# Attention and two feed-forward layers on one core: output groups six blocks behind, next pair's weights in sequence, its input parts behind product 7

## The chip, the cores and the metric

The kernel runs on one core of one Trainium2 chip. The metric is device time in microseconds (us), the median over several executions. Five engines each work through a queue of their own in order: TensorE (PE, matmuls), VectorE (DVE), ScalarE (ACT), GpSimd (POOL) and SyncE (SP, which here issues every DMA transfer).

## The reference

```python
def reference(**kwargs):
    attn_out = _attn_ref(**attn_kwargs)        # causal, window 128, 4 x 8 heads x 576 x 64
    x = np.ascontiguousarray(attn_out.transpose(0, 2, 1, 3)).reshape(B * S, H * D)   # 2304 x 512
    x = _moe_ref(x=x, **moe_kwargs)            # (silu(x @ w_gate) * (x @ w_val)) @ w_out, 1536 wide
    return _moe2_ref(x=x, **moe2_kwargs)       # h = x @ w_in; (h * tanh(softplus(h))) @ w_out, 2048 wide
```

All of it is fp32. The first feed-forward layer is called layer 1 below, the second layer 2.

## The kernel before

Every fp32 operand of a large matmul is kept as two halves, a high one that ACT writes (a copy to the type fp32r, `hi_act`) and a low one that DVE writes (the difference, `lo_dve`). One logical matmul is three on PE: high x high, high x low, low x high.

**Layer 1** runs over five chunks of tokens (`A_CHUNKS`, the last has 384). For each of 12 blocks of the hidden width, `gv_groups` makes 24 matmuls into two of four rotating PSUM banks (gate and value; ACT and DVE read them and write the halves `hh`, `hl`), and `out_group` makes 12 matmuls that add the block to the four output banks `acc0` to `acc3`. Output groups run some blocks behind: the last chunk's by `CFG["lastlag"]`. Those that are left when the last block is done (the list `carry`) run on PE just before layer 2. Their weights come in six `ring` tiles of two blocks each, read back from DRAM (`cw<-w1od`) and split by ACT and DVE; two of them fit at a time. After the last output group the four banks are copied out (`ev`).

While the last chunk runs, `combos` prepares layer 2's output weights for eight column blocks: it loads one (`cw<-w2d`), takes four differences on POOL, splits seven parts into halves (`chl`, ACT and DVE) and stores them to DRAM (`w2o<-chl`).

**Layer 2** takes 2x2 blocks by seven products in place of eight (a scheme of the Strassen kind), in three pairs of 384-token tiles. Per pair, `hidden` is called for j = 0 to 7, each with seven products of six matmuls on the input's seven parts `xs1` to `xs7` and the weight tile `win` of j. `make_win` makes `win`: four differences on POOL in the one tile `t4`, then high and low halves by ACT and DVE, in two pieces of 768 and 1024 columns, from the raw weights that `load_raw` fetches (`w<-w2d`, two buffers). Then come the output products in the order `ORDER2` = 4, 1, 6, 7, 2, 5, 3. Each consists of four operands `op` (halves of the hidden values `G`; five buffers) and 12 matmuls per operand, with weights `wout` loaded 1 MB at a time into three buffers. `x_parts` makes the next pair's `xs` from `xr`, its input as loaded from `x2d`: seven high halves on ACT, seven low halves on DVE and four sums on DVE. `win` and `xr` take turns in three buffers of one tag.

PE's order is the program's own. The queues of the other engines are filled by a scheduler that takes what its own clock says is ready first; the kernel gives it priorities and, with `tc.issue_after`, single orders. In the loop over pairs `x_parts` and `make_win` of the next pair stand among the output products:

```python
if p + 1 < NPB:
    if i == 7:
        xs = x_tiles(br, range(1, 8))
        x_parts(xs, xr)
    if i in (2, 5):
        j = (2, 5).index(i)
        make_win(p + 1, j)
        load_raw(p + 1, j + 2)
```

Of the kernel before, what the change touches and what calls it, by code (L numbers as in the profile page):

```python
# [9 lines left out]
F32 = mybir.dt.float32  # L10
F32R = mybir.dt.float32r
# [3 lines left out]
AF = mybir.ActivationFunctionType  # L15
ALU = mybir.AluOpType
# [8 lines left out]
A_CHUNKS = [512, 384, 512, 512, 384]  # L25
S_FULL = [4, 4, 0, 0, 0]
TB = 384
NPB = NT // (2 * TB)
NJ = NF2 // 2

SLOT = {1: 0, 2: 1, 3: 2, 5: 3, 6: 4, 7: 5, 4: 6}
CFG = dict(
    order="SSOTT", delay0=2, early=[4], pbufs=10, pump_g=2, pump_p=2, lag=4, lastlag=3, evprio=500,
    conv_a=0.1, conv_b=0.9,
)

# [60 lines left out]
def body(ctx: ExitStack, tc: tile.TileContext, qT, kT, vP, w1, w1o, w2, cst, yT):  # L97
    nc = tc.nc
# [10 lines left out]
    w2d = dr.tile([NF2, 128, 1024], F32, name="w2d")  # L109
# [11 lines left out]


    def hi_act(out, in_):
        nc.scalar.activation(out=out, in_=in_, func=AF.Copy)  # L124

    def lo_dve(out, in_, hi):
        nc.vector.tensor_tensor(out=out, in0=in_, in1=hi.bitcast(F32), op=ALU.subtract)  # L127

    plansA = []
    t = 0  # L130
# [165 lines left out]
    early = {}  # L296
# [219 lines left out]
    def conv_w2(i):  # L516
# [10 lines left out]

        steps(("w2d", i), [f0] + [lambda k=k: raw["f"][k]() for k in range(5)] + [f6])

    def combos(b):  # L530

        st = {}

        def f0():
            st["w"] = bpool["p"].tile([128, 8, 256], F32, tag="cw8", name="cw8")
            nc.sync.dma_start(out=st["w"][:, 0:4], in_=w2d[b].rearrange("p (k n) -> p k n", k=4))

        def f1():
            w = st["w"]
            for o, x, y in ((4, 0, 1), (5, 3, 4), (6, 3, 0), (7, 5, 2)):  # L540
                nc.gpsimd.tensor_tensor(out=w[:, o], in0=w[:, x], in1=w[:, y], op=ALU.subtract)  # L541

        def half(e):
            st[e] = bpool["p"].tile([128, 7, 256], F32R, tag="chl", name="chl", bufs=3)
            return st[e]

        def f2():
            hi_act(half(0), st["w"][:, 1:8])

        def f3():  # L550
            lo_dve(half(1), st["w"][:, 1:8], st[0])

        def f4():
            for e in range(2):
                h = st[e].bitcast(F32)
                nc.sync.dma_start(out=w2o[:, :, b - NJ, e].rearrange("s p n -> p s n"), in_=h)

        steps(("c", b), [f0, f1, f2, f3, f4])
# [34 lines left out]
    def gv_groups(ci, i):  # L593
        p = plansA[ci]
        n = p.n
        st = {}

        def g():
            need(("w", i))
            st["g"] = hid(x_t[ci], n, wt[i], 0)  # L600
            t = hp_.tile([128, 512], F32, tag="t", name="t")
            tanhs.append(nc.scalar.activation(out=t[:, :n], in_=st["g"][:, :n], func=AF.Tanh, scale=0.5))  # L602
            nc.vector.scalar_tensor_tensor(  # L603
                out=t[:, :n], in0=t[:, :n], scalar=1.0, in1=st["g"][:, :n], op0=ALU.add, op1=ALU.mult
            )
            st["t"] = t

        def v():
            vps = hid(x_t[ci], n, wt[i], 512)
            t = st["t"]  # L610
            nc.vector.scalar_tensor_tensor(  # L611
                out=t[:, :n], in0=t[:, :n], scalar=0.5, in1=vps[:, :n], op0=ALU.mult, op1=ALU.mult
            )
            if ci == len(plansA) - 1:
                hh = bpool["p"].tile([128, 512], F32R, tag="hhb", name="hh", bufs=CFG["lastlag"] + 2)
                hl = bpool["p"].tile([128, 512], F32R, tag="hlb", name="hl", bufs=CFG["lastlag"] + 2)
            else:
                hh = hp_.tile([128, 512], F32R, tag="hh", name="hh", bufs=2)
                hl = hp_.tile([128, 512], F32R, tag="hl", name="hl", bufs=2)
            hi_act(hh[:, :n], t[:, :n])  # L620
            lo_dve(hl[:, :n], t[:, :n], hh[:, :n])
            hs["A", ci, i] = (hh, hl)

        return [g, v]
# [29 lines left out]
    def bank():  # L654
# [3 lines left out]
            return rot("bk")  # L658
        return ps.tile([128, 512], F32, tag=f"acc{c % CT}", name="bk", bufs=1)

    def part(x, src):
        hi_act(x[:, 0], src)
        lo_dve(x[:, 1], src, x[:, 0])

    def add(out, a, b, op=ALU.add):
        nc.vector.tensor_tensor(out=out, in0=a, in1=b, op=op)  # L666
# [20 lines left out]
    def x_tiles(bp, which):  # L687
        return {i: bp.tile([128, 2, 2, TB], F32R, tag=f"xs{i}", name=f"xs{i}", bufs=1) for i in which}
# [50 lines left out]
    def layer2(br):  # L739
# [9 lines left out]
        def load_raw(p, j):  # L749
            raws[p, j] = br.tile([128, 4, 256], F32, tag="w4", name="w4", bufs=2)  # L750
            nc.sync.dma_start(out=raws[p, j], in_=w2d[j].rearrange("p (k n) -> p k n", k=4))

        def make_win(p, j):

            w = raws.pop((p, j))
            x = t4
            for o, a, b in ((0, w[:, 0], w[:, 1]), (1, w[:, 3], x[:, 0]), (2, w[:, 3], w[:, 0]), (3, x[:, 1], w[:, 2])):
                nc.gpsimd.tensor_tensor(out=x[:, o], in0=a, in1=b, op=ALU.subtract)  # L758
            t = win[p, j] = br.tile([128, 2, 7, 256], F32R, tag="win", name="win")
            for d, src in ((slice(0, 3), w[:, 1:4]), (slice(3, 7), x)):  # L760
                hi_act(t[:, 0, d], src)
                lo_dve(t[:, 1, d], src, t[:, 0, d])
# [62 lines left out]
        for p in range(NPB):  # L825
            loads = [(i, k) for i in ORDER2 for k in range(2)]
            for j in range(NJ):
                if j + 2 < NJ:
                    make_win(p, j + 2)
                if j + 4 < NJ:  # L830
                    load_raw(p, j + 4)
                if j >= NJ - 3:
                    load_wout(p, *loads.pop(0))
                hidden(p, j, xs)
            if p + 1 < NPB:
                xr = load_x(br, p + 1)
                for j in range(2):
                    load_raw(p + 1, j)
            us = [{}, {}]
            ys = [[bp.tile([128, 2, TB], F32, tag="y", name="y", bufs=4) for _ in range(2)] for _ in range(2)]  # L840
            held = {}
            left = [[2, 2], [2, 2]]
            t0 = 2 * p * TB
            for i in ORDER2:
                bks = held[i] = held[onto2[i]] if i in onto2 else [bank(), bank()]
                for q, o in enumerate(operands(p, i)):
                    k, jq = divmod(2 * q, NJ // 2)
                    if (p, i, k) not in wout:
                        load_wout(p, i, k)
                        loads.remove((i, k))  # L850
                    w = wout[p, i, k]
                    if jq == 0 and loads:
                        load_wout(p, *loads.pop(0))
                    for m in range(2):
                        products(
                            bks[m],
                            [(w[:, jq + e, 0, 128 * m:128 * m + 128], w[:, jq + e, 1, 128 * m:128 * m + 128]) for e in range(2)],
                            [(o[:, 0, e], o[:, 1, e]) for e in range(2)],
                            i not in onto2 and q == 0, i not in onto2.values() and q == NJ // 2 - 1,
                        )  # L860
                for m in range(2):

                    def done(k, a, b, m=m):
                        t, f = divmod(k, 2)
                        y = ys[f][m]
                        if b is None:
                            nc.scalar.activation(out=y[:, t], in_=a, func=AF.Copy)
                        else:
                            add(y[:, t], a, b, ALU.subtract if k == 2 else ALU.add)
                        left[f][m] -= 1  # L870
                        if not left[f][m]:
                            nc.sync.dma_start(out=yr[:, 2 * f + m, t0:t0 + 2 * TB], in_=y.rearrange("p a t -> p (a t)"))

                    def new():
                        return bp.tile([128, TB], F32, tag="u", name="v", bufs=6)

                    if i == 4:
                        us[m]["p4"] = bks[m][:, :TB]
                        continue
                    outputs(i, bks[m], us[m], new, done, False)  # L880
                    if i == 7:
                        done(2, us[m]["b"], us[m]["p4"])
                if p + 1 < NPB:
                    if i == 7:
                        xs = x_tiles(br, range(1, 8))
                        x_parts(xs, xr)
                    if i in (2, 5):
                        j = (2, 5).index(i)
                        make_win(p + 1, j)
                        load_raw(p + 1, j + 2)  # L890

    with tc.manual_schedule(engines={mybir.EngineType.PE}):
        nc.sync.dma_start(out=cst_sb, in_=cst)
# [162 lines left out]
```

## Time and profile before

| what | value |
| --- | --- |
| median of 3 runs | 1024.19 us (1022.73 to 1025.08) |
| the profiled execution | 1022.81 us, of which the span of the trace is 1021.0 us |
| TensorE busy | 982.3 us, 96% of the span |
| VectorE busy | 704.1 us, 69% |
| ScalarE busy | 550.5 us, 54% |
| GpSimd busy | 183.2 us, 18% |
| mean granted TensorE clock | 0.986 of full |

A group of the trace's rows gives start, duration, engine, line and the tiles written and read; in square brackets stands the idle time of the engine before it and what ended that. The granted clock is a share of TensorE's full speed.

### The profile page before, as it was taken

How to read it: one execution, taken by the hardware profiler on the slowest of the kernel's cores; microseconds unless marked ns; L12 is line 12 of the kernel's file. 1: busy time of each engine (PE TensorE's matmuls, PEld its weight loads, DVE VectorE, ACT ScalarE, POOL GpSimd, SP SyncE). 2: the span in 40 equal slices, each digit the busy share in tenths (PEclk: the TensorE clock that was granted, in tenths of full speed). 3: DMA queues.
4: the chain of work that ended last, by engine and by line, in shares of the span. 5: the costliest groups of instructions: out<-in, count | busy, mean ns of one | idle time of the engine just before them, and what ended most of it. 6: DMA issues, size and time to landing. Idle time of an engine off the chain costs nothing.

```text
span 1021.0 us, 14513 instructions
## 1 busy us (share of the span) xinstructions
PE 982.3 (96%) x5168; PEld 861.5 (84%) x5168; DVE 704.1 (69%) x1247; ACT 550.5 (54%) x1121; POOL 183.2 (18%) x204
## 2 busy tenths in 40 slices
PE   7899999999999999999999999599999999999998
PEld 5566777899987777787888999599899998999998
DVE  5988887777667644558643666877974888757773
ACT  6867565767666654545543345456453564335442
POOL 3700000000000000000002342542821429113000
PEclk9989999999999999999999999799999999999999
DMA  8844423476354622336401997513685236850275
GB/s 314 287 193 134 158 80 115 146 245 204 84 186 142 225 84 61 110 111 235 159 22 63 329 367 257 210 63 104 226 288 187 83 121 231 292 160 21 69 258 189
DMA packets 74936, 173.90 MB, mean 170 GB/s; under 512 B 8432, under 2 KB 50032, under 8 KB 65136
## 3 DMA queue, kind: packets, MB, share of 16 engines
q1 hardware_dynamic: 74864, 172.98, 51.0%
q8 instruction: 40, 0.66, 0.2%
q14 instruction: 32, 0.26, 0.1%
HBM read 137.30 MB, written 35.65 MB: 169 GB/s over the span
## 4 chain that ended last, share of the span: by engine, by line
PE 77%; DVE 8%; DMA 5%; POOL 5%; ACT 2%; issue 2%; SPq 1%; DVEq 0%; ACTq 0%; POOLq 0%
PE g_ps L117 28%; PE bk L117 24%; PE acc L117 14%; PE o_ps L117 5%; POOL t L758 4%; PE s_ps L117 4%; PE t_ps L259 3%; DMA wout<-w2o 2%; DVE G L666 1%; DVE win L127 1%; DMA wraw<-w 1%; DVE op L127 1%; POOL Pt L249 1%; DVE xs L127 1%; DVE xr L666 1%
## 5 line engine op out<-in xcount | busy, mean ns | idle before, releaser
L117 PE MATMUL g_ps<-xt,w 128*128 128x512 f32 (+1 forms) x1440 | 322.2, 375 | 0.3 <-ACT PT L271 0.3
L117 PEld LDWEIGHTS g_ps<-xt,w 128*128 128x128 f32 x1440 | 259.5, 188 | 40.3 <-issue 3.3
L117 PE MATMUL bk<-xs,win 128*128 128x384 f32 x1008 | 179.4, 337 | 14.2 <-ACT xs L124 8.0
L117 PEld LDWEIGHTS bk<-xs,win 128*128 128x128 f32 x1008 | 176.4, 189 | 16.9 <-ACT xs L124 8.3
L117 PE MATMUL bk<-op,wout 128*128 128x384 f32 x1008 | 180.9, 340 | 6.4 <-DVE op L127 4.9
L117 PEld LDWEIGHTS bk<-op,wout 128*128 128x128 f32 x1008 | 177.6, 191 | 9.2 <-DVE op L127 6.7
L117 PE MATMUL acc<-hh,ring 128*128 128x512 f32 (+1 forms) x480 | 149.7, 374 | 0.0
L758 POOL TENSOR_TENSOR t<-w 128x256 f32<-128x256 f32 x48 | 82.3, 1735 | 195.6 <-DVE win L127 184.5
L117 PEld LDWEIGHTS acc<-hh,ring 128*128 128x128 f32 x480 | 89.0, 188 | 13.8 <-issue 1.9
L124 ACT ACTIVATE op<-G 128x768 fp32r<-128x768 f32 x84 | 69.1, 841 | 47.3 <-PE bk L117 44.1
L127 DVE TENSOR_TENSOR op<-G,op 128x768 fp32r<-128x768 f32 x84 | 79.5, 957 | 21.7 <-ACT op L124 21.6
L117 PE MATMUL acc<-hl,ring 128*128 128x512 f32 (+1 forms) x240 | 88.4, 368 | 0.0
L230 ACT ACTIVATE Pt<-Pt,sm 128x256 f32<-128x256 f32 (+2 forms) x160 | 74.6, 467 | 16.7 <-DVE sm L226 16.3
L226 DVE CUSTOM_DVE_ANT_0 Pt<-s_ps,cst_sb 128x256 f32<-128x256 f32 (+2 forms) x160 | 54.3, 376 | 34.9 <-PE s_ps L117 34.8
L602 ACT ACTIVATE t<-g_ps 128x512 f32<-128x512 f32 (+1 forms) x60 | 33.1, 551 | 78.3 <-PE g_ps L117 78.3
L603 DVE SCALAR_TENSOR_TENSOR t<-t,g_ps 128x512 f32<-128x512 f32 (+1 forms) x60 | 37.7, 628 | 52.5 <-ACT t L602 52.4
L611 DVE SCALAR_TENSOR_TENSOR t<-t,g_ps 128x512 f32<-128x512 f32 (+1 forms) x60 | 37.9, 632 | 43.6 <-PE g_ps L117 42.7
L209 POOL MEMSET sm<- 128x8 f32 x40 | 5.3, 144 | 338.4 <-ACT Pt L247 310.2
L541 POOL TENSOR_TENSOR cw<-cw 128x256 f32<-128x256 f32 x32 | 30.4, 971 | 192.7 <-DMA cw<-w2d 192.2
L666 DVE TENSOR_TENSOR G<-u,bk 128x384 f32<-128x384 f32 x72 | 39.3, 553 | 36.0 <-PE bk L117 33.8
L1001 ACT ACTIVATE G<-G 128x384 f32<-128x384 f32 x72 | 37.0, 519 | 49.3 <-DVE G L666 49.3
L124 ACT ACTIVATE hh<-t 128x512 fp32r<-128x512 f32 (+1 forms) x60 | 34.9, 582 | 52.6 <-DVE t L611 52.6
(71 smaller groups left out, 1313.3 us busy)
## 6 DMA issues: line engine op xcount, KB each, us to landing
wout<-w2o SPq DMA_DIRECT2D x42, 1024.0 KB, 5.4
wraw<-w SPq DMA_DIRECT2D x16, 1024.0 KB, 5.4
w2o<-chl SPq DMA_DIRECT2D x16, 896.0 KB, 5.9
wst<-w SPq DMA_DIRECT2D x12, 1024.0 KB, 8.0
cw<-w1od SPq DMA_DIRECT2D x24, 512.0 KB, 4.0
w<-w2d SPq DMA_DIRECT2D x24, 512.0 KB, 3.4
w2d<-cw SPq DMA_DIRECT2D x16, 512.0 KB, 3.6
wraw<-w1o SPq DMA_DIRECT2D x6, 1024.0 KB, 6.0
```

The lines of the kernel that those rows point to most:

```text
L117: nc.tensor.matmul(out=out, lhsT=lhsT, rhs=rhs, start=start, stop=stop, skip_group_check=True)
L124: nc.scalar.activation(out=out, in_=in_, func=AF.Copy)
L127: nc.vector.tensor_tensor(out=out, in0=in_, in1=hi.bitcast(F32), op=ALU.subtract)
L226: nc.vector.tensor_tensor_reduce(out=Pt[:q.qn, :w], in0=s_ps[:q.qn, q.so:q.so + w], in1=nb[:q.qn, 128 - q.kn:128 + q.qn], op0=ALU.add, op1 ...
L230: nc.scalar.activation(out=Pt[:q.qn, :w], in_=Pt[:q.qn, :w], func=AF.Exp, scale=-1.0, bias=sm[:q.qn, i:i + 1], accum_out=sm[:q.qn, 8 + i:9 ...
L259: nc.tensor.transpose(t_ps[:x.n, o:o + q.qn], Pt[:q.qn, c0:c0 + x.n], ident[:q.qn, :q.qn])
L602: tanhs.append(nc.scalar.activation(out=t[:, :n], in_=st["g"][:, :n], func=AF.Tanh, scale=0.5))
L603: nc.vector.scalar_tensor_tensor(out=t[:, :n], in0=t[:, :n], scalar=1.0, in1=st["g"][:, :n], op0=ALU.add, op1=ALU.mult)
L611: nc.vector.scalar_tensor_tensor(out=t[:, :n], in0=t[:, :n], scalar=0.5, in1=vps[:, :n], op0=ALU.mult, op1=ALU.mult)
L666: nc.vector.tensor_tensor(out=out, in0=a, in1=b, op=op)
L758: nc.gpsimd.tensor_tensor(out=x[:, o], in0=a, in1=b, op=ALU.subtract)
L1001: nc.scalar.activation(out=out, in_=in_, func=AF.Mish)
```

## The change

The last chunk's output groups run six blocks behind, not three; the buffers of `hh` and `hl` are cut to the chunk's 384 columns (eight buffers of each, not five). `combos` writes its differences to a tile of its own with one buffer, so that its two kinds of columns are split in two instructions on each of ACT and DVE. In layer 2 `make_win` and `load_raw` run on in sequence over the pair's end: the next pair's j = 0 and 1 are made in this pair's j = 6 and 7. `x_parts` is tied behind the last two operations that made the operands of product 7 (`latest`).

```diff
--- before.py
+++ after.py
@@ -30,7 +30,7 @@
 
 SLOT = {1: 0, 2: 1, 3: 2, 5: 3, 6: 4, 7: 5, 4: 6}
 CFG = dict(
-    order="SSOTT", delay0=2, early=[4], pbufs=10, pump_g=2, pump_p=2, lag=4, lastlag=3, evprio=500,
+    order="SSOTT", delay0=2, early=[4], pbufs=10, pump_g=2, pump_p=2, lag=4, lastlag=6, evprio=500,
     conv_a=0.1, conv_b=0.9,
 )
 
@@ -121,10 +121,10 @@
 
 
     def hi_act(out, in_):
-        nc.scalar.activation(out=out, in_=in_, func=AF.Copy)
+        return nc.scalar.activation(out=out, in_=in_, func=AF.Copy)
 
     def lo_dve(out, in_, hi):
-        nc.vector.tensor_tensor(out=out, in0=in_, in1=hi.bitcast(F32), op=ALU.subtract)
+        return nc.vector.tensor_tensor(out=out, in0=in_, in1=hi.bitcast(F32), op=ALU.subtract)
 
     plansA = []
     t = 0
@@ -527,28 +527,39 @@
 
         steps(("w2d", i), [f0] + [lambda k=k: raw["f"][k]() for k in range(5)] + [f6])
 
+    def differences(w, x):
+        for o, a, b in ((0, w[:, 0], w[:, 1]), (1, w[:, 3], x[:, 0]), (2, w[:, 3], w[:, 0]), (3, x[:, 1], w[:, 2])):
+            nc.gpsimd.tensor_tensor(out=x[:, o], in0=a, in1=b, op=ALU.subtract)
+
+    def parts7(w, x):
+        return (slice(0, 3), w[:, 1:4]), (slice(3, 7), x)
+
     def combos(b):
 
         st = {}
 
         def f0():
-            st["w"] = bpool["p"].tile([128, 8, 256], F32, tag="cw8", name="cw8")
-            nc.sync.dma_start(out=st["w"][:, 0:4], in_=w2d[b].rearrange("p (k n) -> p k n", k=4))
+            st["w"] = bpool["p"].tile([128, 4, 256], F32, tag="cw4", name="cw4")
+            nc.sync.dma_start(out=st["w"], in_=w2d[b].rearrange("p (k n) -> p k n", k=4))
 
         def f1():
             w = st["w"]
-            for o, x, y in ((4, 0, 1), (5, 3, 4), (6, 3, 0), (7, 5, 2)):
-                nc.gpsimd.tensor_tensor(out=w[:, o], in0=w[:, x], in1=w[:, y], op=ALU.subtract)
+            x = st["x"] = bpool["p"].tile([128, 4, 256], F32, tag="ct4", name="ct4", bufs=1)
+            differences(w, x)
 
         def half(e):
             st[e] = bpool["p"].tile([128, 7, 256], F32R, tag="chl", name="chl", bufs=3)
             return st[e]
 
         def f2():
-            hi_act(half(0), st["w"][:, 1:8])
+            h = half(0)
+            for d, src in parts7(st["w"], st["x"]):
+                hi_act(h[:, d], src)
 
         def f3():
-            lo_dve(half(1), st["w"][:, 1:8], st[0])
+            l = half(1)
+            for d, src in parts7(st["w"], st["x"]):
+                lo_dve(l[:, d], src, st[0][:, d])
 
         def f4():
             for e in range(2):
@@ -612,8 +623,8 @@
                 out=t[:, :n], in0=t[:, :n], scalar=0.5, in1=vps[:, :n], op0=ALU.mult, op1=ALU.mult
             )
             if ci == len(plansA) - 1:
-                hh = bpool["p"].tile([128, 512], F32R, tag="hhb", name="hh", bufs=CFG["lastlag"] + 2)
-                hl = bpool["p"].tile([128, 512], F32R, tag="hlb", name="hl", bufs=CFG["lastlag"] + 2)
+                hh = bpool["p"].tile([128, A_CHUNKS[-1]], F32R, tag="hhb", name="hh", bufs=CFG["lastlag"] + 2)
+                hl = bpool["p"].tile([128, A_CHUNKS[-1]], F32R, tag="hlb", name="hl", bufs=CFG["lastlag"] + 2)
             else:
                 hh = hp_.tile([128, 512], F32R, tag="hh", name="hh", bufs=2)
                 hl = hp_.tile([128, 512], F32R, tag="hl", name="hl", bufs=2)
@@ -658,9 +669,10 @@
             return rot("bk")
         return ps.tile([128, 512], F32, tag=f"acc{c % CT}", name="bk", bufs=1)
 
+    latest = []
+
     def part(x, src):
-        hi_act(x[:, 0], src)
-        lo_dve(x[:, 1], src, x[:, 0])
+        latest[:] = hi_act(x[:, 0], src), lo_dve(x[:, 1], src, x[:, 0])
 
     def add(out, a, b, op=ALU.add):
         nc.vector.tensor_tensor(out=out, in0=a, in1=b, op=op)
@@ -825,17 +837,14 @@
         for p in range(NPB):
             loads = [(i, k) for i in ORDER2 for k in range(2)]
             for j in range(NJ):
-                if j + 2 < NJ:
-                    make_win(p, j + 2)
-                if j + 4 < NJ:
-                    load_raw(p, j + 4)
+                for f, k in ((make_win, p * NJ + j + 2), (load_raw, p * NJ + j + 4)):
+                    if k < NPB * NJ:
+                        f(*divmod(k, NJ))
                 if j >= NJ - 3:
                     load_wout(p, *loads.pop(0))
                 hidden(p, j, xs)
             if p + 1 < NPB:
                 xr = load_x(br, p + 1)
-                for j in range(2):
-                    load_raw(p + 1, j)
             us = [{}, {}]
             ys = [[bp.tile([128, 2, TB], F32, tag="y", name="y", bufs=4) for _ in range(2)] for _ in range(2)]
             held = {}
@@ -880,14 +889,11 @@
                     outputs(i, bks[m], us[m], new, done, False)
                     if i == 7:
                         done(2, us[m]["b"], us[m]["p4"])
-                if p + 1 < NPB:
-                    if i == 7:
-                        xs = x_tiles(br, range(1, 8))
+                if p + 1 < NPB and i == 7:
+                    xs = x_tiles(br, range(1, 8))
+                    with tc.issue_after(latest[0].ins), tc.issue_after(latest[1].ins):
                         x_parts(xs, xr)
-                    if i in (2, 5):
-                        j = (2, 5).index(i)
-                        make_win(p + 1, j)
-                        load_raw(p + 1, j + 2)
+
 
     with tc.manual_schedule(engines={mybir.EngineType.PE}):
         nc.sync.dma_start(out=cst_sb, in_=cst)
```

The first place is PE's queue in the last chunk of layer 1, before; `g_ps` is a gate or value group, `acc_5548` the first output bank.

```order
L117 MATMUL acc_4534<-hh,ring 128x512
L117 MATMUL g_ps<-xt,w 128x384 x72
L117 MATMUL acc_5548<-hh,ring 128x384
L117 MATMUL acc_5548<-hl,ring 128x384
L117 MATMUL acc_5548<-hh,ring 128x384
```

The same place in the changed kernel:

```order
L117 MATMUL acc_4534<-hh,ring 128x512
L117 MATMUL g_ps<-xt,w 128x384 x144
L117 MATMUL acc_5693<-hh,ring 128x384
L117 MATMUL acc_5693<-hl,ring 128x384
L117 MATMUL acc_5693<-hh,ring 128x384
```

Three more blocks (72 matmuls) now run ahead of the first output group, and so three more output groups stand behind the last block.

The second place is DVE's queue between layer 1 and layer 2, before, from the last `hl`; of the `xs` names 6026 is `xs1`, 6029 `xs2`, 6027 `xs4`, 6022 `xs5`, 6021 `xs7`, 6028 `xs6`, 6030 `xs3`.

```order
L127 TENSOR_TENSOR win<-w_6018,win 128x768
L127 TENSOR_TENSOR xs_6026<-xr,xs_6026 128x768
L127 TENSOR_TENSOR xs_6029<-xr,xs_6029 128x768
L581 COPY ev<-acc_5549 128x384
L127 TENSOR_TENSOR win<-t_6020,win 128x1024
L581 COPY ev<-acc_5551 128x384
L127 TENSOR_TENSOR xs_6027<-xr,xs_6027 128x768
L127 TENSOR_TENSOR win<-w_6031,win 128x768
L666 TENSOR_TENSOR xr<-xr 128x768 x3
```

The same place in the changed kernel (6009 is `xs1`, 6012 `xs2`, 6010 `xs4`):

```order
L127 TENSOR_TENSOR win<-w_6001,win 128x768
L127 TENSOR_TENSOR xs_6009<-xr,xs_6009 128x768
L127 TENSOR_TENSOR xs_6012<-xr,xs_6012 128x768
L127 TENSOR_TENSOR win<-t_6003,win 128x1024
L127 TENSOR_TENSOR ring<-cw,ring 128x1024
L127 TENSOR_TENSOR xs_6010<-xr,xs_6010 128x768
L127 TENSOR_TENSOR win<-w_6014,win 128x768
L678 TENSOR_TENSOR xr<-xr 128x768 x2
L592 COPY ev<-acc_5694 128x384
```

The first copy of an output bank now stands behind five more instructions of layer 2 (and one `ring`), which before stood behind it.

The third place is DVE's queue at the end of the first pair's hidden part, before; `w_6671` and `w_6673` are the next pair's weights, and `xs_6971` and so on its input parts.

```order
L127 TENSOR_TENSOR win<-w_6671,win 128x768
L127 TENSOR_TENSOR win<-t_6020,win 128x1024
L666 TENSOR_TENSOR u<-u,bk 128x384
L127 TENSOR_TENSOR xs_6971<-xr,xs_6971 128x768
L666 TENSOR_TENSOR u<-u,bk 128x384
L666 TENSOR_TENSOR G<-u,bk 128x384 x2
L127 TENSOR_TENSOR xs_6972<-xr,xs_6972 128x768
L666 TENSOR_TENSOR G<-u,bk 128x384
L127 TENSOR_TENSOR xs_6974<-xr,xs_6974 128x768
L127 TENSOR_TENSOR op<-G,op 128x768
```

In the changed kernel the last four `xs` stand here, near the end of the output part (`xs_7019` is `xs3`, the last of the seven):

```order
L127 TENSOR_TENSOR xs_7023<-xr,xs_7023 128x768
L127 TENSOR_TENSOR op<-G,op 128x768
L678 TENSOR_TENSOR xr<-xr 128x768
L127 TENSOR_TENSOR op<-G,op 128x768
L127 TENSOR_TENSOR xs_7022<-xr,xs_7022 128x768
L127 TENSOR_TENSOR op<-G,op 128x768 x2
L127 TENSOR_TENSOR xs_7019<-xr,xs_7019 128x768
L127 TENSOR_TENSOR op<-G,op 128x768 x2
```

The seven parts have moved from before and among the operands of products 4 to 7 to places among those of products 2, 5 and 3; two operands still stand behind the last part.

## Rows read from the trace of the kernel before

**Rows 1.** Waits of PE from 560 us on: total, times, longest.

```profile
PE bk L117 <- DVE op L127: 4.9, 4, 2.0
PE bk L117 <- DVE G L666: 2.2, 6, 0.5
PE bk L117 <- DMA wout<-w2o: 1.5, 2, 1.0
```

**Rows 2.** Timeline of PE through layer 2: start, duration, instruction, idle time before it.

```profile
637.02 1.22 PE L117 MATMUL bk<-xs,win 128*128 128x384 f32 x6
646.20 0.69 PE L117 MATMUL bk<-xs,win 128*128 128x384 f32 x1 [7.95 <-ACT xs L124]
...
711.02 19.37 PE L117 MATMUL bk<-op,wout 128*128 128x384 f32 x109
732.37 14.47 PE L117 MATMUL bk<-op,wout 128*128 128x384 f32 x72 [1.99 <-DVE op L127]
...
774.28 20.99 PE L117 MATMUL bk<-xs,win 128*128 128x384 f32 x120
...
833.85 19.38 PE L117 MATMUL bk<-op,wout 128*128 128x384 f32 x109
...
898.35 20.99 PE L117 MATMUL bk<-xs,win 128*128 128x384 f32 x120
...
957.94 50.11 PE L117 MATMUL bk<-op,wout 128*128 128x384 f32 x288
```

**Rows 3.** Chain that ended last, at the last chunk's end: start, duration, work.

```profile
622.54 2.08 PE acc L117 x12
624.63 4.24 PE g_ps L117 x24
```

**Rows 4.** Timeline of all engines between the two layers.

```profile
616.57 1.71 ACT L124 ACTIVATE chl<-cw 128x1792 fp32r<-128x1792 f32 x1 [1.88 <-DMA w2o<-chl]
...
620.82 0.71 SPq L751 DMA_DIRECT2D w<-w2d  x1
...
629.49 0.53 ACT L124 ACTIVATE hh<-t 128x384 fp32r<-128x384 f32 x1 [0.85 <-DVE t L611]
...
630.66 1.56 ACT L124 ACTIVATE xs<-xr 128x768 fp32r<-128x768 f32 x2
...
636.18 0.56 DVE L581 COPY ev<-acc 128x384 f32<-128x384 f32 x1 [2.62 <-PE acc L117]
...
636.65 1.22 DVE L127 TENSOR_TENSOR win<-t,win 128x1024 fp32r<-128x1024 f32 x1
...
638.25 1.23 DVE L127 TENSOR_TENSOR xs<-xr,xs 128x768 fp32r<-128x768 f32 x1
...
639.41 1.47 DVE L127 TENSOR_TENSOR win<-w,win 128x768 fp32r<-128x768 f32 x1
...
640.81 3.86 DVE L666 TENSOR_TENSOR xr<-xr 128x768 f32<-128x768 f32 x3
...
650.92 1.33 PE L117 MATMUL bk<-xs,win 128*128 128x384 f32 x3 [4.03 <-DVE xs L127]
```

**Rows 5.** Windows: us, busy of PE, PEld, DVE, ACT, POOL, PEclk, DMA share, GB/s.

```profile
600.00:610.00 10.00, 10.00 (x59) 10.00 (x58) 5.83 (x8) 5.58 (x6) 3.07 (x4) 1.00 1.04 346
...
615.00:620.00 5.00, 5.00 (x30) 5.00 (x30) 2.84 (x4) 2.11 (x2) 1.46 (x2) 1.00 0.46 159
```

**Rows 6.** The same windows view, two stretches after a wait of PE.

```profile
652.00:655.00 3.00, 3.00 (x12) 3.00 (x12) 2.09 (x4) 1.79 (x2) 0.00 (x0) 0.58 0.00 0
...
732.40:735.00 2.60, 2.60 (x10) 2.60 (x11) 2.60 (x4) 1.43 (x2) 2.60 (x1) 0.62 0.05 19
```

**Rows 7.** Timeline of all engines in the first pair's output part.

```profile
719.36 20.32 POOL L758 TENSOR_TENSOR t<-w 128x256 f32<-128x256 f32 x2 [8.63 <-DVE win L127]
...
741.23 1.06 ACT L124 ACTIVATE win<-t 128x1024 fp32r<-128x1024 f32 x1 [6.29 <-POOL t L758]
```

## The prediction

> **What bounds the kernel now.** I read the engines' shares first: TensorE is busy for 96% of the span, so only its waits can be won. The list of its waits from 560 us on is short. Two long ones lie between the layers, 7.95 and 4.03 us, both for input parts `xs` [rows 2, 4]. Then come operands of the output products (4.9 us in four waits), hidden values `G` (2.2 us in six) and output weights (1.5 us in two) [rows 1]. The timeline of PE gives the stretches. Between the layers PE ends product 1 at 638.24 (637.02 + 1.22) and runs steadily again only at 650.92, with one matmul between. The output part of the first pair runs from 711.02 to 774.28, 63.26 us; of the second from 833.85 to 898.35, 64.50 us. That of the third, which has no next pair to prepare, does 288 matmuls in 50.11 us, so 336 would take 58.46 us [rows 2]. The two that prepare a successor lose 4.80 + 6.04 = 10.84 us beside it.
>
> **Part 1, three more blocks of lag.** Nothing is removed on PE; it is reordered. An output group takes 2.08 us and a block's 24 gate and value matmuls 4.24 us [rows 3]. Three more groups behind the last block let it end 3 x 2.08 = 6.24 us earlier, while the last output group ends where it did. What hangs on the last block comes earlier: its `hh` on ACT at 629.49, and the first two `xs` at 630.66 right behind [rows 4]. PE's wait shrinks by as much as the chain to `xs6` (product 6 is the second) moves.
>
> Bounds for the start of those `xs`. Early: 630.66 - 6.24 = 624.4, and 1.2 us more for a `ring` split that now stands ahead (priced like the 128x1024 `win` of 1.22 us [rows 4]): 625.6. Late: no earlier than now, if the data sets it. The loads of `w` and `xr` are issued from 620.82, behind the last stores of `combos`, and the last `chl` itself waited 1.88 us for such a store [rows 4]. The DMA engines were full from 600 to 610 (share 1.04), and had room only from 615 to 620 (0.46) [rows 5]. That room is 0.54 x 5 = 2.7 us. I take it as what the loads can move up, since the bytes stay the same: `xs` from 628.0.
>
> From there to product 6, DVE's work sets the time. Now it is 650.92 - 630.66 = 20.26 us, of which 2.62 us is DVE waiting for PE's second output bank before it may copy it out [rows 4]. In the changed queue that copy stands behind five more instructions of layer 2, so I drop the 2.62 and add one `ring` of 1.22: 18.86 us, and product 6 runs from 628.0 + 18.9 = 646.9. The gain is 650.92 - 646.9 = **4.0 us**. From 630.66 it would be 649.5 (gain 1.4). From 625.6 the copy of the bank bounds it. Of the 14.74 us from the copy (636.18) to product 6, the order moves ahead 1.22 + 1.23 + 1.47 and two thirds of 3.86, together 6.5 us [rows 4]; that gives 636.18 + 8.24 = 644.4, gain 6.5. PE still idles for over 8 us, and the stretch at 0.58 of the clock behind the wait [rows 6] stays, so I credit none of that.
>
> The split of `chl` into two instructions costs ACT little: 0.78 (half of 1.56) + 1.06 for 1.71 us, eight times 0.13, with ACT busy 5.6 of 10 us there [rows 4, 5, 7]. The cover is the four rotating banks: PE can be two blocks, 8.5 us, ahead of ACT. The differences' single buffer makes POOL wait for DVE's `chl`; that cost is in the late bound.
>
> **Part 2, the next pair's weights and input.** At each of two pair ends, ACT and DVE lose two `make_win` and seven input parts from the early output part, which is where PE waited 1.99 us for an operand at 732.37 [rows 2]. Behind that wait the granted clock was 0.62 of full, between its two levels of 1.2 and 2.4 GHz, and only 10 matmuls started in 2.6 us, where 15 would at the third pair's rate [rows 2, 6]. So each pair end loses more than its waits. Of the 10.84 us, one wait of up to 1.0 us is for output weights [rows 1], and I do not credit it: 9.84 us.
>
> What it adds: `make_win` for j = 6 and 7 now runs in the hidden part. Blocks j = 0 to 5 of each pair carry one already, and PE waits there for `G` six times, 2.2 us in three pairs [rows 1]; one more of 0.37 us in each of two pairs costs 0.7. Net **9.1 us**.
>
> Are the moved parts hidden? An operand lasts 58.46 / 28 = 2.09 us on PE, and with five buffers the 16th (the last of product 7) is written when the 11th is done, 23 us into the output part. The `xs` begin there. The last one stands behind operand 26, whose buffer comes free with the 21st, at 43.9 us, and ahead of the last two operands. So it is done about 10 us before the next pair starts at 58.5. If that cover were gone, what is late costs PE its own length, some 1.3 us for each part or sum [rows 4]. The transfer of `xr` now has to wait for the buffer of j = 7, that is for the end of the hidden part; it has 23 us, and `w` and `xr` together took under 9.84 us from issue to use [rows 4]. On SP the output weights stand behind it: the fourth, needed 6 x 2.09 = 12.5 us in, waits with it, but `xr` is issued as soon as the hidden part ends. A queue in which it sat longer would cost PE just that excess.
>
> **The sum.** 1022.81 (profiled) - 4.0 - 9.1 = 1009.7. The median of the three runs stands 1.38 us above the profiled execution, which is one of the quicker ones; half of that added, I predict 1010.4.
>
> **The rivals.** A, *the data is not earlier*: DMA and the single difference buffer hold the loads where they are. For it: the full DMA and the 1.88 us wait [rows 4, 5]; against it: the room at 615. Then 1022.81 - 1.4 - 9.1 = 1012.3.
>
> B, *half a pair end*: the wait of 1.99 us moves to another operand, as DVE must now also pass the parts among the operands of products 2, 5 and 3. Against it: an operand is due only every 2.09 us, five buffers deep. 1022.81 - 4.0 - 4.6 = 1014.2.
>
> C, *all of it*: 6.5 between the layers and 10.84 at the pair ends, if the data is early and the output weights no longer wait: 1005.5.
>
> D, *slower, by a blocked POOL*: at 719.36 two differences took 20.32 us while DVE worked without a pause, and ACT stood 6.29 us for them [rows 7]. The changed program puts such a `make_win` into j = 7, and on ACT the last `G` and operands stand behind it. Three operands (6.3 us) are ready by then. If POOL is stuck for 20.32 us there, PE waits 14 us at each pair end: 1009.7 + 28 = 1037.8. Break-even is at 6.3 + 6.6 = 12.9 us of POOL time. Against it: blocks with a `make_win` wait only for `G`, at most 0.5 us [rows 1], and POOL's differences for j + 2 are not due for two blocks.
>
> The Trainium skill ("SBUF — State Buffer", section "Who interferes with whom") says that a DVE instruction with two SBUF inputs and a GpSimd instruction that reads SBUF take turns under an exclusive lock, and that the later one is blocked fully. The trace agrees: 20.32 us [rows 7]. By that rule every added `make_win` in a crowded block would block one engine or the other, which is rival D, and the sum 1037.8; by the rows of the blocks that have one it is the 0.7 us above.
>
> E, *nothing*: what is won is lost to new waits, 1022 to 1024.
>
> **Chances.** My forecast (1006.5 to 1011.5 and a little over) 40%, A 17%, B 17%, C 14%, E 5%, D and other losses 7%. About 0.2%, 2 us, is what a measurement of this kernel can tell from no change. So faster 0.88, same 0.05, slower 0.07. The range from 1004 to 1017 holds the forecast, A, B and most of C, and leaves out D and E.
>
> **What would show it.** Right: PE's wait between the layers is 7 to 9 us and no longer 12; both output parts of pairs 1 and 2 last 58.5 to 60 us, with no wait for an operand and a full clock; the hidden parts grow by under 1 us; POOL's differences stay near 3 us for four. Part 1 is wrong if the first `xs` on ACT is not earlier than 630, or if PE waits inside the last chunk, where ACT would stand at a `chl`. Part 2 is wrong if PE waits at a pair's start for `xs`, or among products 2, 5 and 3 for an operand, or if the output weights land late behind `xr`. The whole is wrong if ACT stands long for POOL in j = 6 or 7.

## The result, and the profile after

The changed kernel takes 1009.58 us (median of four runs, 1008.53 to 1012.78) against 1024.63 us; the ratio over all executions is 0.9865, with an interval of 0.9847 to 0.9883. The forecast was 1010.4 us. The profiled execution is the slowest of the four (1012.78 us, span 1010.7). In it even the last matmul of the 512-column chunks, which runs ahead of the last chunk's output groups in both kernels, starts at 569.50 us, before at 565.34. That 4.2 us of lateness carries through, so I compare stretches, not absolute times.

PE's waits from 555 us on (total, times, longest), and PE's timeline through layer 2 (start, duration, instruction, idle time before it), of the changed kernel:

```profile
PE bk L117 <- DVE xs L127: 4.3, 1, 4.3
PE bk L117 <- DVE G L678: 2.7, 8, 0.5
PE bk L117 <- ACT xs L124: 2.7, 1, 2.7
PE bk L117 <- DMA wout<-w2o: 1.1, 1, 1.1
```

```profile
641.07 1.23 PE L117 MATMUL bk<-xs,win 128*128 128x384 f32 x6
645.02 0.44 PE L117 MATMUL bk<-xs,win 128*128 128x384 f32 x1 [2.73 <-ACT xs L124]
649.74 21.99 PE L117 MATMUL bk<-xs,win 128*128 128x384 f32 x113 [4.28 <-DVE xs L127]
672.25 14.86 PE L117 MATMUL bk<-xs,win 128*128 128x384 f32 x84 [0.52 <-DVE G L678]
...
710.82 58.43 PE L117 MATMUL bk<-op,wout 128*128 128x384 f32 x336
769.09 20.99 PE L117 MATMUL bk<-xs,win 128*128 128x384 f32 x120
...
829.25 58.43 PE L117 MATMUL bk<-op,wout 128*128 128x384 f32 x336
887.51 20.99 PE L117 MATMUL bk<-xs,win 128*128 128x384 f32 x120
...
947.10 50.11 PE L117 MATMUL bk<-op,wout 128*128 128x384 f32 x288
998.30 8.59 PE L117 MATMUL bk<-op,wout 128*128 128x384 f32 x48 [1.09 <-DMA wout<-w2o]
```

The four waits for an operand [rows 1] are gone. Each output part of pairs 1 and 2 is now one row of 336 matmuls: from its start to the next pair's it lasts 58.27 and 58.26 us, before 63.26 and 64.50 [rows 2]. Between the layers PE starts product 1 at 641.07 and runs steadily from 649.74, so 8.67 us later; before it was 650.92 - 637.02 = 13.90. The wait is shorter, and it is still there.

What stands in it is in the timeline of SP, ACT and DVE of the changed kernel:

```profile
620.63 1.35 SPq L694 DMA_DIRECT2D xr<-x2d  x2
...
628.78 1.06 ACT L124 ACTIVATE ring<-cw 128x1024 fp32r<-128x1024 f32 x1 [0.97 <-PE acc L117]
629.75 0.83 ACT L124 ACTIVATE win<-w 128x768 fp32r<-128x768 f32 x1
...
630.49 1.56 ACT L124 ACTIVATE xs<-xr 128x768 fp32r<-128x768 f32 x2
...
637.32 1.49 DVE L127 TENSOR_TENSOR win<-w,win 128x768 fp32r<-128x768 f32 x1
638.73 2.90 DVE L678 TENSOR_TENSOR xr<-xr 128x768 f32<-128x768 f32 x2
...
646.82 1.47 DVE L678 TENSOR_TENSOR xr<-xr 128x768 f32<-128x768 f32 x1
648.21 2.34 DVE L127 TENSOR_TENSOR xs<-xr,xs 128x768 fp32r<-128x768 f32 x2
```

The first `xs` start at 630.49, that is 10.58 us before product 1 (before: 637.02 - 630.66 = 6.36 [rows 2, 4]). DVE then works almost without a pause until `xs6` is there, 19.25 us later.

### The profile page after: what moved, and what is told of

The parts are those of the page before. It is cut to its first block, busy times and chain, and to the rows that moved or that the text cites. A ratio compares the mean times of both kernels' runs of the same rounds, so it can differ in the third digit from the quotient of the medians.

```text
span 1010.7 us, 14521 instructions
## 1 busy us (share of the span) xinstructions
PE 979.5 (97%) x5168; PEld 859.5 (85%) x5168; DVE 701.3 (69%) x1255; ACT 552.1 (55%) x1129; POOL 135.4 (13%) x204
## 4 chain that ended last, share of the span: by engine, by line
PE 84%; DVE 6%; DMA 5%; ACT 2%; issue 2%; POOL 1%; SPq 1%; DVEq 0%; POOLq 0%
PE bk L117 29%; PE g_ps L117 28%; PE acc L117 13%; PE o_ps L117 6%; PE s_ps L117 4%; PE t_ps L259 3%; DVE G L678 1%; DVE win L127 1%; DMA wout<-w2o 1%; DMA xr<-x2d 1%; DMA wraw<-w 1%; POOL Pt L249 1%; DMA wst<-w 1%; DMA w2d<-cw 1%; DVE xs L127 1%
## 5 line engine op out<-in xcount | busy, mean ns | idle before, releaser
L117 PE MATMUL bk<-op,wout 128*128 128x384 f32 x1008 | 175.6, 334 | 1.1 <-DMA wout<-w2o 1.1
L117 PEld LDWEIGHTS bk<-op,wout 128*128 128x128 f32 x1008 | 174.8, 188 | 1.4 <-issue 1.4
L117 PEld LDWEIGHTS acc<-hh,ring 128*128 128x128 f32 x480 | 89.0, 188 | 13.8 <-issue 1.9
L230 ACT ACTIVATE Pt<-Pt,sm 128x256 f32<-128x256 f32 (+2 forms) x160 | 74.5, 467 | 16.9 <-DVE sm L226 16.4
L770 POOL TENSOR_TENSOR t<-w 128x256 f32<-128x256 f32 x48 | 42.6, 907 | 230.8 <-DVE win L127 217.5
L247 ACT ACTIVATE Pt<-Pt,sm 128x256 f32<-128x256 f32 (+2 forms) x128 | 50.2, 465 | 7.9 <-DVE sm L241 7.8
L127 DVE TENSOR_TENSOR hl<-t,hh 128x512 fp32r<-128x512 f32 (+1 forms) x60 | 39.7, 662 | 20.7 <-ACT hh L124 20.3
```

What stands on the lines that cost most here:

```text
L117: nc.tensor.matmul(out=out, lhsT=lhsT, rhs=rhs, start=start, stop=stop, skip_group_check=True)
L127: return nc.vector.tensor_tensor(out=out, in0=in_, in1=hi.bitcast(F32), op=ALU.subtract)
L230: nc.scalar.activation(out=Pt[:q.qn, :w], in_=Pt[:q.qn, :w], func=AF.Exp, scale=-1.0, bias=sm[:q.qn, i:i + 1], accum_out=sm[:q.qn, 8 + i:9 ...
L247: nc.scalar.activation(out=pt, in_=pt, func=AF.Copy, scale=r)
```

## The experiments

The gains in us below are the ratio's distance from 1 times 1024.

**Part 1 alone**: the kernel before with `lastlag` 6, the shorter `hh` and `hl`, and the new `combos`; layer 2 as before.

```diff
-    ... lag=4, lastlag=3, ...
+    ... lag=4, lastlag=6, ...
```

> The kernel before with part 1 alone (lag of six, narrower hh and hl, the differences in a tile of their own); layer 2 as before. My theory: what hangs on the last block comes 4 us earlier against TensorE's end of the output groups, so the stretch from that end to the steady start of product 6 falls from 13.9 us to about 8.7, as in the changed kernel; the pair ends stay at 63.3 and 64.5 us; the time falls by 4 to 5.5 us (ratio 0.9945 to 0.996). Rival (the data sets the start): the stretch stays over 12 us and the time falls by 1.4 us or less (ratio over 0.9985).

Measured: ratio 0.9962 (0.9946 to 0.9978), a gain of 3.9 us. The stretches come from a further profile of the same kernel:

> The same kernel as the run of part 1 alone, for a profile at full clock. From product 1's start to the steady start of product 6: 8.5 to 9.5 us if the lag does all of it as in the changed kernel; over 10 us if half of what the changed kernel shows there is of another origin. The output parts last 63 to 64.5 us as before.

```profile
637.97 1.22 PE L117 MATMUL bk<-xs,win 128*128 128x384 f32 x6
641.93 0.44 PE L117 MATMUL bk<-xs,win 128*128 128x384 f32 x1 [2.74 <-ACT xs L124]
646.65 22.02 PE L117 MATMUL bk<-xs,win 128*128 128x384 f32 x113 [4.28 <-DVE xs L127]
```

That is PE's timeline of this further profile: 646.65 - 637.97 = 8.68 us, as in the changed kernel. Part 1 does all of what is seen between the layers; the next run shows that within it the lag does. The output parts stay at 64.43 and 64.54 us.

**The changed kernel with the old lag**: `lastlag` 3, all else as changed.

> The changed kernel with the last chunk's output groups three blocks behind again, everything else as changed (buffers cut, combos with the tile of its own). If all of part 1's gain is the lag and the split of combos costs nothing: as the run of part 2 alone, ratio 0.990 (0.989 to 0.991), and the wait between the layers from product 1 to the steady start of product 6 is 13 to 14 us, as before. If the split in combos costs something that the lag hides: ratio 0.992 or more. If the lag is worth only 1.4 us (rival A): ratio 0.988.

Measured: ratio 0.9903 (0.9886 to 0.9919); product 1 to the steady start is 651.79 - 637.89 = 13.90 us, exactly as before, in PE's timeline of this run:

```profile
637.89 1.22 PE L117 MATMUL bk<-xs,win 128*128 128x384 f32 x6
...
651.79 21.69 PE L117 MATMUL bk<-xs,win 128*128 128x384 f32 x113 [4.04 <-DVE xs L127]
```

The ratio is the level of part 2 alone, so the new `combos` with its two split instructions costs nothing that shows. The lag is worth 0.9903 - 0.9865, again 3.9 us, with an uncertainty of some 2.5.

**Part 2 alone, and its two halves.** First the whole of it (`make_win` and `load_raw` in sequence, `x_parts` tied), then only the tie, then only the sequence:

```diff
+                    with tc.issue_after(latest[0].ins), tc.issue_after(latest[1].ins):
                         x_parts(xs, xr)
```

```diff
-                if j + 2 < NJ:
-                    make_win(p, j + 2)
-                if j + 4 < NJ:
-                    load_raw(p, j + 4)
+                for f, k in ((make_win, p * NJ + j + 2), (load_raw, p * NJ + j + 4)):
+                    if k < NPB * NJ:
+                        f(*divmod(k, NJ))
```

> The kernel before with part 2 alone (weights in sequence over the pair's end, input parts behind product 7); lag of three, differences as before. My theory: the two output parts with a successor last 58.3 to 59 us, the stretch between the layers stays at 13.9 us, and the time falls by 9 to 10 us (ratio 0.990 to 0.9915); with part 1 alone it adds up to the whole change, 14 to 15 us. Rival: the two parts help each other or get in each other's way, so that the sum is off by over 2 us.

> The kernel before with the input parts tied behind product 7's operands, and nothing else; the next pair's weights are written where they were. My theory (the seven input parts and four sums in the early output part are what makes PE wait there): nearly all of part 2, 8 to 10 us less, output parts of 58.3 to 59.5 us, and POOL's 20 us stretch goes, since VectorE is no longer busy without a pause. Rival (the weights are the cause: ScalarE stands 6.3 us for POOL in a make_win): under 3 us less, and the 20 us stretch of POOL stays.

> The kernel before with the weights in sequence over the pair's end, and the input parts not tied. My theory: VectorE still makes the input parts among the operands of products 4 to 7, so PE still waits for operands at each pair end, though less, since two make_win are out of the way: output parts of 60.5 to 63 us, time 2 to 5 us less. Rival (the weights are the cause): output parts of 58.3 to 59.5 us, time 8 to 10 us less.

Measured: both halves 0.9899 (0.9879 to 0.992), 10.3 us; the tie alone 0.9889 (0.9867 to 0.9912), 11.4 us; the sequence alone 0.9908 (0.9888 to 0.9927), 9.4 us. Whole and parts multiply: 0.9962 x 0.9899 = 0.9861, for 0.9865 measured. But the halves of part 2 do not add. Either one removes the whole loss at the pairs' ends, as PE's timelines of the first pair's output part show, the tie alone first, then the sequence alone:

```profile
713.00 58.43 PE L117 MATMUL bk<-op,wout 128*128 128x384 f32 x336
771.26 20.99 PE L117 MATMUL bk<-xs,win 128*128 128x384 f32 x120
```

```profile
712.41 50.24 PE L117 MATMUL bk<-op,wout 128*128 128x384 f32 x288
...
771.79 20.99 PE L117 MATMUL bk<-xs,win 128*128 128x384 f32 x120
```

My expectation for the sequence alone was wrong. So the loss is not simply the amount of moved work. Two causes could both have been removed by either half: DVE, which has too much to do ahead of some operand, and GpSimd, whose differences took 20.32 us (I call them stuck) and held ACT [rows 7]. Five runs, all edits of the kernel before, tell these apart.

**Without GpSimd's differences, first try**: left out in the two `make_win` written into the pair's end.

```diff
-                        make_win(p + 1, j)
+                        make_win(p + 1, j, False)
```

> The kernel before; only the GpSimd differences of the two make_win at each pair's end are left out (those two weight tiles hold stale differences). DVE's and ACT's queues are the same in content and order. Theory 1 (GpSimd, stuck 20.3 us behind a DVE that works without a pause, holds ACT and with it the operands): both output parts fall from 63.3 and 64.5 to 58.3 to 59.5 us, ratio 0.989 to 0.992, like the halves. Theory 2 (DVE and ACT simply have too much work there, whatever GpSimd does): the parts stay at 61.5 to 64.5 us, ratio 0.996 to 1.0. In between (60 to 61.5 us, ratio 0.992 to 0.996): both.

Measured: ratio 1.0003 (0.9994 to 1.0013). But the test missed its mark, as GpSimd's and ACT's timeline of this run shows:

```profile
721.21 20.32 POOL L759 TENSOR_TENSOR t<-w 128x256 f32<-128x256 f32 x2 [30.36 <-DVE win L127]
...
743.07 1.06 ACT L124 ACTIVATE win<-t 128x1024 fp32r<-128x1024 f32 x1 [6.29 <-POOL t L759]
```

The stuck differences are still there. They belong to the next `make_win`, that of the new pair's j = 2, which the scheduler had pulled into the output part. All that this run shows is that the differences which I left out cost nothing.

**Without the differences that were stuck**: left out for j = 2 of the second and third pair.

```diff
+            if p == 0 or j != 2:
                 for o, a, b in (...): nc.gpsimd.tensor_tensor(...)
```

> The kernel before, without GpSimd's four differences in the one make_win (j = 2 of the second and third pair) whose first two took 20.32 us and held ACT for 6.29 us (those two weight tiles hold stale differences; the first pair's end keeps its order on DVE and ACT). Theory 2 (DVE's work alone makes the wait for the tenth operand): that wait stays at 2.0 us, the half clock behind it stays, only the later one of 0.47 us goes; first output part 62.5 to 63, ratio 0.998 to 1.0. Theory 1 (GpSimd stuck): part 58.3 to 60, ratio 0.989 to 0.993.

Measured: ratio 0.9981 (0.9968 to 0.9995), the output parts 62.05 and 60.83 us. PE's timeline of this run in the first pair's output part:

```profile
712.75 19.36 PE L117 MATMUL bk<-op,wout 128*128 128x384 f32 x109
734.10 31.31 PE L117 MATMUL bk<-op,wout 128*128 128x384 f32 x179 [1.99 <-DVE op L127]
766.40 8.56 PE L117 MATMUL bk<-op,wout 128*128 128x384 f32 x48 [0.99 <-DMA wout<-w2o]
```

The wait for the tenth operand stays at 1.99 us to the hundredth, with GpSimd idle. That wait is DVE's. What goes is the later one of 0.46 us, behind ACT's stand, and the slow matmuls behind the first wait; that the half clock would stay was wrong. From the first output part to the end of PE it is 301.70 us, before 306.14: GpSimd is worth 4.4 us in the trace of this one execution and 1.9 us (0.5 to 3.3) by the ratio of them all, and nothing like 10. Some 3.7 of the 4.4 us are the 72 matmuls behind the first wait of each pair, now at the full clock (179 in 31.31 us, so 72 in 12.6; before 14.47 [rows 2]). Why the clock stays up is open (last section).

**Less work for DVE, in three doses**: the four sums of `x_parts` at the pairs' ends cover 288, 192 and 96 of the 384 tokens, the rest stays unsummed.

```diff
+            return [a[:, :, :288] if short else a for a in aps]
...
-        add(a22, a21, a22)
+        add(*cut(a22, a21, a22))
...
-                        x_parts(xs, xr)
+                        x_parts(xs, xr, True)
```

> The kernel before; each of the four sums of x_parts at the pairs' ends covers 288 of the 384 tokens (the rest of xr stays unsummed). If DVE's work alone sets it, 4 x 0.2 = 0.8 us less work ahead of the tenth operand makes the wait for it 1.2 us instead of 2.0. If GpSimd sets it: unchanged at 2.0.

> As the run with 288, with 192 of 384 tokens: 4 x 0.4 = 1.6 us less work; the wait for the tenth operand is 0.4 us by DVE's work alone, and a wait that short would leave the clock up: output part about 59.5, ratio 0.992 to 0.994. By GpSimd: 2.0 and 63.

> As the run with 288, with 96 of 384 tokens: 4 x 0.6 = 2.4 us less work; no wait for the tenth operand by DVE's work alone, output parts 58.3 to 59, ratio 0.990 to 0.992, though GpSimd's differences may still take long. By GpSimd: 2.0 and 63.

Measured: the wait for the tenth operand falls with the first two doses, from 1.99 to 1.43 and 0.66 us, and not with the third, 0.74 us (the scheduler also swaps a few instructions, in the last run most). GpSimd alone would have left it at 2.0, DVE's work alone taken it to 1.2, 0.4 and none. The ratios miss what I expected: 1.0001 (0.9987 to 1.0015), 0.9974 (0.9957 to 0.9991) and 0.9973 (0.9959 to 0.9988). PE's timeline of the run with 288, then two rows of the run with 192:

```profile
734.90 10.51 PE L117 MATMUL bk<-op,wout 128*128 128x384 f32 x59 [1.43 <-DVE op L127]
```

```profile
728.96 10.70 PE L117 MATMUL bk<-op,wout 128*128 128x384 f32 x60 [0.66 <-DVE op L127]
741.59 2.36 PE L117 MATMUL bk<-op,wout 128*128 128x384 f32 x12 [1.94 <-DVE op L127]
```

The run with 96 shows why the time hardly falls, in the timeline of all engines:

```profile
718.03 17.39 POOL L760 TENSOR_TENSOR t<-w 128x256 f32<-128x256 f32 x2 [8.29 <-DVE win L127]
...
729.84 10.70 PE L117 MATMUL bk<-op,wout 128*128 128x384 f32 x60 [0.74 <-DVE op L127]
...
736.96 1.06 ACT L124 ACTIVATE win<-t 128x1024 fp32r<-128x1024 f32 x1 [5.77 <-POOL t L760]
737.92 3.76 ACT L124 ACTIVATE op<-G 128x768 fp32r<-128x768 f32 x5
...
741.61 2.38 PE L117 MATMUL bk<-op,wout 128*128 128x384 f32 x12 [1.08 <-DVE op L127]
...
744.43 0.79 PE L117 MATMUL bk<-op,wout 128*128 128x384 f32 x3 [0.44 <-DVE op L127]
```

PE, less held up at the tenth operand, now runs into ACT's stand of 5.77 us: the five operands queued behind it come late. In the run with 192 that second wait is 1.94 us. So the two causes lie one behind the other, and taking out DVE's uncovers GpSimd's. The table has one profiled execution of each kernel:

| kernel | first output part, us | second, us | first output part to PE's end, us |
| --- | --- | --- | --- |
| before | 63.26 | 64.50 | 306.14 |
| less DVE work (96 tokens) | 62.29 | 62.56 | 304.27 |
| GpSimd's stuck differences out | 62.05 | 60.83 | 301.70 |
| sequence alone | 59.38 | 58.68 | 296.14 |
| tie alone | 58.26 | 58.40 | 295.52 |
| changed kernel | 58.27 | 58.26 | 296.07 |

No run takes out both causes at once; that together they are the whole loss is read from the traces of the two halves, not measured. The tie takes `xs` and their sums from in front of the tenth operand; and since DVE then pauses for ACT, GpSimd gets through earlier, as DVE's and GpSimd's timeline of that run shows:

```profile
719.04 9.90 POOL L759 TENSOR_TENSOR t<-w 128x256 f32<-128x256 f32 x2 [7.05 <-DVE win L127]
...
725.83 1.82 DVE L127 TENSOR_TENSOR op<-G,op 128x768 fp32r<-128x768 f32 x2
728.71 1.05 DVE L127 TENSOR_TENSOR op<-G,op 128x768 fp32r<-128x768 f32 x1 [1.06 <-ACT op L124]
```

On ACT nothing stands for GpSimd there any more. The sequence takes the weight tiles' low halves from in front of the tenth operand (0.95 + 1.22 us for one tile), and it leaves no difference on GpSimd between 711.41 and 748.77. By these traces each half removes both causes. With the sequence alone DVE still works 16.0 of the 17 us from 711 on, and all 19 of the next 19, with `xs` among its operands, and PE waits for none of them. The windows view of that run (columns as in [rows 5]):

```profile
711.00:728.00 17.00, 17.00 (x100) 17.00 (x99) 15.97 (x20) 10.47 (x15) 0.41 (x1) 1.00 0.73 242
728.00:747.00 19.00, 19.00 (x112) 19.00 (x111) 19.00 (x23) 12.90 (x17) 0.00 (x0) 1.00 0.80 258
```

**Another order between the layers**, on top of the changed kernel: `x_parts` makes `xs6` right behind the three sums, then 7, 5 and 2, the last sum and 3, and the second weight tile is tied behind them.

```diff
+            for i, a in ((7, a21), (5, a22), (2, a12)):
+                with tc.issue_after(latest[0].ins), tc.issue_after(latest[1].ins):
+                    part(xs[i], a)
...
         x_parts(xs, xr, True)
+        with tc.issue_after(latest[0].ins), tc.issue_after(latest[1].ins):
+            make_win(0, 1)
```

> The changed kernel with another order between the layers alone: the first pair's parts in the order 1, 4, three sums, 6, 7, 5, 2, last sum, 3, and the second weight tile behind them. If the 19 us from the first xs to product 6 are DVE's instructions in front of xs6 (7.5 us of them not needed by product 6): product 6 runs 1.5 to 2.5 us behind product 1's end, not 7, and the time is 2.5 to 5 us under the changed kernel's, ratio 0.9815 to 0.984. If the copies of the output banks, or data, set that wait: ratio 0.986 to 0.987, no gain.

Measured: 1004.02 us (1003.68 to 1006.7), ratio 0.981 (0.9794 to 0.9826), the fastest kernel here. PE's timeline of this run, and its windows (columns as in [rows 5]):

```profile
638.82 1.41 PE L117 MATMUL bk<-xs,win 128*128 128x384 f32 x7
640.78 5.32 PE L117 MATMUL bk<-xs,win 128*128 128x384 f32 x29 [0.55 <-DVE xs L127]
646.94 14.83 PE L117 MATMUL bk<-xs,win 128*128 128x384 f32 x84 [0.83 <-ACT win L124]
664.21 16.40 PE L117 MATMUL bk<-xs,win 128*128 128x384 f32 x84 [2.44 <-DVE G L678]
```

```profile
649.00:652.00 3.00, 3.00 (x19) 2.97 (x18) 2.90 (x5) 0.99 (x2) 2.66 (x3) 1.00 1.00 419
...
664.00:667.00 3.00, 2.79 (x9) 2.79 (x10) 1.18 (x3) 1.55 (x3) 2.61 (x4) 0.56 0.00 0
```

PE waits 0.55 us for `xs`, and a little later 0.83 us for `win`, in place of 2.73 + 4.28. The clock stays at its full level, 2.4 GHz, up to 664; in the changed kernel it was at or near the level of 1.2 GHz from 649 to 655:

```profile
649.00:652.00 3.00, 2.26 (x7) 2.26 (x8) 2.09 (x3) 1.58 (x3) 0.00 (x0) 0.50 1.01 421
652.00:655.00 3.00, 3.00 (x13) 3.00 (x12) 2.49 (x4) 0.38 (x1) 0.90 (x2) 0.60 1.00 395
655.00:658.00 3.00, 3.00 (x19) 3.00 (x18) 1.11 (x2) 1.15 (x3) 1.97 (x3) 1.00 0.42 165
```

So the order of the parts in DVE's and ACT's queues sets the wait that the lag left over, not data and not the output banks. What is put off comes late: PE waits 2.44 us for `G` at 664.21, with DVE then behind its work. Behind that wait the granted clock is 0.56, and 84 matmuls take 16.40 us instead of 14.83. From product 1 to the output part it is 705.32 - 638.82 = 66.50 us, in the changed kernel 710.82 - 641.07 = 69.75, and behind it 0.33 us less. So the rows show 3.6 us, the ratios 5.6 with an uncertainty of some 2.5.

## Why the prediction was right, step by step

**The total.** Forecast 13.8 us below the median then shown (1024.19 to 1010.4), measured 1024.63 - 1009.58 = 15.05 by the medians and 13.8 by the ratio, both inside the range. In the traces the two stretches that the change touches give 5.23 + 9.09 = 14.3 us: from product 1 to the steady start, and from there to PE's end (before 1017.16 - 650.92 = 366.24, after 1006.89 - 649.74 = 357.15). The sum had 4.0 + 9.1.

**Part 1: the mechanism held, its size was between 4 and 5 us.** Forecast 4.0; the trace shows 5.23, of which up to 0.5 may be given back by the stretch behind it (21.99 us for 113 matmuls, 21.52 before [rows 2]; the runs with the old lag have 21.36 to 22.65 there, so the difference is within their spread). Both comparisons of times show 3.9 with an uncertainty of about 2. The term that was off is the start of the first `xs`. I took 628.0, 9.0 us before product 1, from the DMA engines' room; it was 10.58, near my early bound of 11.4. The timeline names what ended the idle time: ACT stood for PE's output groups at `ring`, then did `win`, and went on to `xs` without a pause; the half of `xr` that the first `xs` read had landed at 627.9, 7.3 us after its issue (before, at 629.6). Rival A, that the data would not be earlier, is refuted. One of my signs would say otherwise: part 1 was to be wrong if the first `xs` on ACT is not earlier than 630, and it starts at 630.49. The sign was ill chosen, since it is an absolute time, and this execution was 4.2 us late already. In the further profile of part 1 alone the first `xs` starts at 627.38. DVE's chain to product 6 was 19.25 us for 18.86 forecast.

**Part 2: the sum held, its reason was too simple.** The parts fell by 4.99 and 6.24, together 11.23 us; I credited 9.84 and left out 1.0 for output weights, and that wait went too. The hidden parts grew by 0.98 and 0.59 us (60.16 for 59.57 in the second), where I had 0.7 for both together, and 0.47 of the 0.98 is the stretch of 113 matmuls named above. In the third pair a wait for output weights grew from 0.51 to 1.09 us. That makes 11.23 - 0.98 - 0.59 - 0.57 = 9.09. To come out so near to 9.1 is luck: both terms were too small, and the wait in the third pair, which the sum did not have, lies between none and 1.47 us in the runs here. The step that was incomplete is the cause: "ACT and DVE lose two `make_win` and seven input parts". I priced the loss as one, without asking how much of it each half carries. The count was too high, too: in the trace before, DVE's low halves of the first of the two weight tiles (704.82) and two of the seven parts (707.37 and 710.65) run before the output part starts at 711.02. The runs show two causes in a row, DVE 2.0 us late at the tenth operand and ACT held by GpSimd, of which removing one uncovers the other, and which, by the traces, either half of the edit removes together. Rival B, half a pair end, did not come: behind product 7 PE waits for no operand, although DVE passes all seven parts there.

**Rival D**, GpSimd blocked in j = 7, did not come. The differences of the next pair's j = 2 now run at 706.87, in the hidden part, the first two in 1.44 us, and PE's new wait there is 0.22 us. The Trainium skill ("SBUF — State Buffer", "Who interferes with whom") exempts a DVE instruction with at most one SBUF input from the lock, as long as it is not in one of DVE's two-port modes. That fits these traces: in the hidden blocks DVE also reads `bk`, which lies in PSUM, and GpSimd is quick; in the stretch of 20.32 us DVE had only instructions with two SBUF inputs.

## What to carry to other kernels

When one edit takes two loads off a crowded stretch, try each half alone: here either gave all of it. Halves that do not add show that the loss is not one amount of work to be shared out; that causes stood one behind the other took further runs to see. A stuck instruction is to be traced to the call that issued it before it is taken out, since the scheduler may have moved it there. After a gain, look at what stands ahead of the first late part in its producer's queue: another order there gave 5.6 us by the ratios (0.9865 to 0.981), 3.6 in the traces, on top of the change.

## What the runs showed of the hardware

GpSimd's two differences did not take a time of their own beside DVE's two-input instructions; they ended when DVE paused. In the tie alone DVE's work ends at 727.65 and the differences at 728.94; with 96 tokens DVE's at 734.13 and they at 735.42. Both are 1.29 us, after 9.90 and 17.39 us of standing.

The clock did not follow the length of the wait alone. The same wait of 1.99 us at the tenth operand was followed by a granted clock of 0.62, between the levels of 1.2 and 2.4 GHz, in the kernel before [rows 6], and by the full one when GpSimd's stuck differences were out, both in the first pair:

```profile
733.00:738.00 5.00, 3.90 (x22) 3.90 (x23) 5.00 (x7) 3.90 (x6) 0.00 (x0) 1.00 0.37 111
```

That is the windows view of that run. PE's order is the same in both, and why the clock fell in one alone stays open. It matters for the size: 72 matmuls behind that wait took 14.47 us before [rows 2], where 12.5 would do at the pace of the undisturbed part (58.27 us for 336), so about 2 of the 5 us that the first pair end lost are the clock's.
